# A chain of attention and two gated feed-forward layers: values stationary in attention's second product, and the first block's inputs cast straight from PSUM

## The chip, the core and the metric

The kernel runs on one core of one Trainium2 chip. The metric is the device time of one execution in microseconds (us), taken as the median of several runs. A core has five engines that run side by side and wait for each other by semaphores: TensorE (PE, matrix products; its weight loads are listed as PEld), VectorE (DVE), ScalarE (ACT), GpSimd (POOL) and SyncE (SP, which issues most transfers). TensorE reads the fast memory SBUF and writes to PSUM, eight banks of accumulators. A matmul has a stationary operand, which is loaded into the array first, and a moving one, whose columns stream through; the stationary operand's columns become the partitions of the result.

## What is computed

Local attention on 4 x 8 heads of 768 positions and 64 features, then two gated layers on the 3072 x 512 result. Cut to what matters:

```python
for c in range(nc):                       # 24 chunks of 32 queries
    k_full = concat([mem_k, k[l_start:r_end]])     # 8 + 16 + 32 + 8 = 64 keys
    v_full = concat([mem_v, v[l_start:r_end]])
    scores = scale * q_c @ k_full.T
    a = softmax(scores)
    out[c] = a @ v_full                   # the "second product": 32 queries x 64 features
x = out.transpose(0, 2, 1, 3).reshape(3072, 512)
x = (sigmoid(x @ w_gate) * (x @ w_val)) @ w_out    # 512 -> 1536 -> 512
h = x @ w_in                                       # 512 -> 2048 -> 512
return (h * sigmoid(h)) @ w_out2
```

## The kernel before

The tokens are cut into 24 tiles of 128 (t = 0 to 23), four to a block of 512. The products of the layers take x with its features on partitions, so that the input of a block is four pieces (KT = 4) of 128 features x 512 tokens, each split into a high and a low part (`fp32r`); three products of the parts make one product of nearly float32.

Attention of one tile goes through these steps. `att_scores` (or `att_scores_paired` for tiles 1 to 3) forms the scores with 64x32 (or 128x64) stationary pieces of q; `att_soften` takes the maximum off and forms the exponential; `att_sum` and `att_norm` divide by the sum; `att_turn` transposes the result on TensorE, so that keys lie on partitions, and ScalarE copies it to SBUF (`at`). `att_pv` is the second product: 4 chunks x 4 head groups x 2 halves make 32 float32 matmuls. Before, 32 queries of `at` are stationary and the 64 features of `vb` move, so that queries come out on partitions; `place` then transposes 32 x 32 blocks on VectorE into the block's `x32`, which has the features on partitions.

The order on each engine is written out by hand. Tiles 0 to 3 run in a prologue, whose order stands in the string `PROLOGUE` (`sc` scores, `max`, `sub`, `exp`, `sum`, `nm` normalise, `pt` turn, `px` second product, `tr` place; `idle` fills TensorE with matmuls that nobody reads; `rebias`, `join`, `high`, `rest` prepare the first weight units from a 64-bit format). Its `px` tiles share two PSUM buffers (`psp`) with the scores. After it `x_high` casts the four pieces of `x32` on ScalarE and `x_low` forms their low parts on VectorE; then the first projection (`proj_both`, tiles `pg` and `pv`) starts.

The other 20 tiles run beside the first layer. At fixed steps `run_events` issues a "meet" for tile t: the second product of tile t-1, directly behind it the scores of tile t, and then on VectorE the placing of t-1 and the softening of t. The second product and the scores lie in one PSUM tile `sx` of two banks. A last meet (t = 24) has only the second product. Everything TensorE does stands in one queue, so a meet stands between two projections (L360) or behind the output product (L104 to L108).

Of the kernel before, what the change touches and what calls it, by code (L numbers as in the profile page):

```python
# [15 lines left out]
P = 128  # L16
# [23 lines left out]
pt.0 sub.2 exp.2 sum.1 sc.3 nm.1 max.3 px.0 idle.1 sum.2 sub.3 exp.3 load.4 qk.4 nm.2 sum.3  # L40
pt.1 tr.0 rebias.0 pt.2 nm.3 px.1 tr.1 v.4 pt.3 join.0 rebias.1 px.2 px.3 idle.1
high.0 tr.2 tr.3 rest.0 join.1
# [15 lines left out]
def moe_kernel(ctx: ExitStack, tc: tile.TileContext, qh, kh, vh, wg, wv, wo, w2i, w2o, out):  # L58
# [237 lines left out]
    def att_pv(t, px, xt, off):  # L296

        at, vb = at_t.pop(t), v_t.pop(t)
        for c in range(4):
            for j in range(4):  # L300
                for a2 in range(2):
                    r = slice(a2 * 64, a2 * 64 + 64)
                    if t in PAIRED:
                        g = (2 * (c // 2) + j % 2) * P + (c % 2) * 2 * CH + (j // 2) * CH
                    else:
                        g = j * P + c * CH
                    o = px[j * CH : j * CH + CH, a2].rearrange("p (h x) -> p h x", h=2)
                    nc.tensor.matmul(  # L308
                        o[:, :, c * CH : c * CH + CH],
                        at[r, g : g + CH],  # L310
                        vb[r, (4 * c + j) * D : (4 * c + j + 1) * D],
# [4 lines left out]
        def place():  # L316
            nc.vector.transpose(
                out=xt[:, :, off : off + P].rearrange("p (u h) x -> p u h x", u=2),
                in_=px.rearrange("p u (h x) -> p u h x", h=2),
            )  # L320
# [5 lines left out]
    def x32_tile(name):  # L326
        return hold[0].tile([P, KT, 512], F32, tag="x32", name=name, bufs=2)
# [60 lines left out]
    with tc.manual_schedule():  # L388
# [115 lines left out]
        x32[0] = x32_tile("x32_0")  # L504
        steps, pts, last_exp = {}, {}, []
# [5 lines left out]
        def pro(what, i):  # L511
# [24 lines left out]
            elif what == "px":  # L536
                px = ps_p(f"px{i}")[:, :, :256]
                (steps["tr", i],) = att_pv(i, px, x32[0], i * P)
# [16 lines left out]
        psp_cm.__exit__(None, None, None)  # L555
        psy_cm = tc.tile_pool(name="psy", bufs=1, space=PSUM)
        psy.append(psy_cm.__enter__())
        src = x32.pop(0)
        x = [p1.tile([P, 2, 512], F32R, tag="x", name=f"x0_{kt}", bufs=5) for kt in range(KT)]

        def x_high(kt):
            nc.scalar.copy(x[kt][:, 0], src[:, kt])
# [17 lines left out]
        x_low(3)  # L580
        units[2].join()
# [17 lines left out]
        def run_events(i):  # L599
            for what, t in events.get(i, []):  # L600
                if what == "meet":
                    sx = ps_att(f"sx{t}")
                    steps = []
                    if t > n0:
# [3 lines left out]
                        steps += list(att_pv(t - 1, sx[:, :, 256:], x32[bn], jj * P))  # L608
# [657 lines left out]
        for bi, n in enumerate(BLOCKS1[:NB1]):  # L1266
# [3 lines left out]
            for f in range(NF1):  # L1270
# [21 lines left out]
                psg = (ps_y if first else ps_m)(f"pg{bi}_{f}")  # L1292
                if first:
                    psv = ps_y(f"pv{bi}_{f}")
# [81 lines left out]
def _layout(q, k, v, mem_k, mem_v, moe_w_gate, moe_w_val, moe_w_out, moe2_w_in, moe2_w_out):  # L1376
# [27 lines left out]
    def gv(w):  # L1404
        w = w.reshape(2, 2, 2, 2, 32, NF1, P)
        return w.transpose(5, 2, 0, 4, 1, 3, 6).reshape(NF1, P, KT * P)
# [39 lines left out]
```

## Time and profile before

| | |
|---|---|
| median of 3 runs | 1099.98 us (1099.97 to 1100.66) |
| the profiled execution | 1100.55 us |
| its span, first to last instruction | 1098.8 us |
| TensorE busy | 1085.0 us (99%) |
| VectorE busy | 758.0 us (69%) |
| ScalarE busy | 534.1 us (49%) |
| GpSimd busy | 95.0 us (9%) |

A profile is one execution. Shares of busy time are means over stages with different limits; the busy time of matmuls is modelled, so gaps are better read from start times. In the rows below a line such as L308 is line 308 of the kernel before, `out<-in` names the tiles with buffer numbers left out, and x64 is the number of instructions in a group. A float32 matmul is run as two passes, each with its own weight load.

### The profile page before, as it was taken

Reading aid. Unit: us, or ns where it says so; the run is one execution under the profiler, and the core shown is the slowest. Engines: PE = TensorE matmul, PEld = TensorE weight load, DVE = VectorE, ACT = ScalarE, POOL = GpSimd, SP = SyncE. Lnnn points to the kernel's source line nnn. Section 1 sums busy time; section 2 is a strip of 40 time slices with the busy share of each in tenths; the row PEclk is TensorE's granted clock in tenths of the full one; section 3 lists DMA queues with packets and bytes.
Section 4 is the critical chain, followed back from the end, with each engine's and each line's share of the span. In section 5 each row is a group of like instructions: output and inputs, shape, how many; then the busy total and the mean of one; then the engine's idle time right before and its main releaser. Section 6 shows DMA issues by size and latency. Waiting matters only on the chain.

```text
span 1098.8 us, 18989 instructions
## 1 busy us (share of the span) xinstructions
PE 1085.0 (99%) x7580; PEld 888.0 (81%) x7580; DVE 758.0 (69%) x1134; ACT 534.1 (49%) x791; POOL 95.0 (9%) x72
## 2 busy tenths in 40 slices
PE   7999999999999999999999999999999999999998
PEld 4888887888887788888778887888888888888887
DVE  7988877677666666667779967478734489443665
ACT  6767545455545453343445545455344445344542
POOL 0000001001000101011111001110011010011000
PEclk9999999999999999999999999999999999999999
DMA  8888788879788787689999599775665756655651
GB/s 313 272 290 303 265 299 263 289 278 331 291 276 302 257 286 275 231 288 353 339 330 363 182 300 315 265 288 207 233 201 201 274 191 227 210 191 209 218 213 68
DMA packets 106248, 288.03 MB, mean 262 GB/s; under 512 B 8624, under 2 KB 39344, under 8 KB 95408
## 3 DMA queue, kind: packets, MB, share of 16 engines
q1 hardware_dynamic: 105872, 286.43, 74.6%
q8 instruction: 60, 0.98, 0.4%
q10 hardware_dynamic: 288, 0.39, 0.1%
q14 instruction: 28, 0.23, 0.1%
HBM read 210.24 MB, written 76.55 MB: 261 GB/s over the span
## 4 chain that ended last, share of the span: by engine, by line
PE 94%; DVE 3%; ACT 1%; DMA 1%; issue 1%; DVEq 0%; ACTq 0%
PE o L1230 21%; PE c L1066 21%; PE pg L360 11%; PE pv L360 11%; PE y L104 4%; PE y L106 4%; PE y L108 4%; PE sx L308 1%; PE sx L220 1%; PE o_-1_1_6485 L1230 1%; PE o_-1_0_6484 L1230 1%; PE pt L292 1%; PE c_-1_5v L1066 1%; PE c_-1_4g L1066 1%; PE c_-1_3v L1066 1%; PE c_-1_2g L1066 1%
## 5 line engine op out<-in xcount | busy, mean ns | idle before, releaser
L1066 PE MATMUL c<-xp,wr 128*128 128x512 f32 x1008 | 229.6, 389 | 0.4 <-ACT s L1101 0.4
L1230 PE MATMUL o<-gf,wr 128*128 128x512 f32 x1008 | 229.0, 389 | 0.0
L1066 PEld LDWEIGHTS c<-xp,wr 128*128 128x128 f32 x1008 | 189.0, 188 | 40.4 <-ACT s L1101 1.2
L1230 PEld LDWEIGHTS o<-gf,wr 128*128 128x128 f32 x1008 | 189.2, 188 | 39.3
L360 PE MATMUL pv<-x,w 128*128 128x512 f32 x564 | 138.6, 394 | 0.0
L360 PE MATMUL pg<-x,w 128*128 128x512 f32 x564 | 136.4, 391 | 0.4 <-ACT x L96 0.4
L1173 DVE TENSOR_TENSOR gf<-g,gf 128x1024 fp32r<-128x1024 f32 x84 | 103.9, 1240 | 46.3 <-ACT gf L1169 45.9
L1169 ACT CAST gf<-g 128x1024 fp32r<-128x1024 f32 x84 | 88.1, 1053 | 86.8 <-PE o L1230 71.4
L360 PEld LDWEIGHTS pg<-x,w 128*128 128x128 f32 x564 | 105.2, 188 | 23.4 <-ACT x L96 1.5
L360 PEld LDWEIGHTS pv<-x,w 128*128 128x128 f32 x564 | 104.1, 188 | 23.2 <-DVE sg L375 0.5
L1031 DVE TENSOR_TENSOR s<-c,s 128x512 f32<-128x512 f32 x48 | 33.2, 691 | 56.7 <-PE c L1066 52.6
L1106 POOL TENSOR_TENSOR s<-s,s 128x512 f32<-128x512 f32 x24 | 34.3, 1431 | 321.7 <-ACT s L1105 321.7
L1034 DVE TENSOR_TENSOR g<-g,g 128x1024 f32<-128x1024 f32 x48 | 60.4, 1258 | 0.0
L370 ACT ACTIVATE sg<-pg 128x512 f32<-128x512 f32 x48 | 28.6, 596 | 60.1 <-PE pg L360 51.8
L380 DVE TENSOR_TENSOR g<-sg,g 128x512 fp32r<-128x512 f32 x48 | 33.2, 692 | 31.8 <-ACT g L377 31.8
L1037 ACT ACTIVATE g<-s 128x512 f32<-128x512 f32 x48 | 30.4, 632 | 50.9 <-DVE s L1031 50.9
L377 ACT CAST g<-sg 128x512 fp32r<-128x512 f32 x48 | 29.8, 620 | 49.3 <-DVE sg L375 49.3
L1031 DVE TENSOR_TENSOR u<-c,s 128x512 f32<-128x512 f32 x24 | 16.6, 690 | 51.8 <-PE c L1066 44.7
L269 ACT ACT_TABLE_LOAD x21 | 26.9, 1283 | 31.5 <-DVE e L261 29.7
L671 POOL TENSOR_TENSOR tcv<-w 128x512 f32<-128x512 f32 x12 | 16.7, 1415 | 284.2 <-DVE fcg L634 284.2
L104 PE MATMUL y<-g,wor 128*128 128x512 f32 x144 | 40.0, 400 | 0.0
L375 DVE TENSOR_TENSOR sg<-pv,sg 128x512 f32<-128x512 f32 x48 | 32.9, 685 | 8.5 <-PE pv L360 6.4
(603 smaller groups left out, 1600.8 us busy)
## 6 DMA issues: line engine op xcount, KB each, us to landing
wr<-w2o_d SPq DMA_DIRECT2D x42, 1024.0 KB, 4.9
wr<-w2i_d SPq DMA_DIRECT2D x24, 1024.0 KB, 5.5
wor<-wo_d SPq DMA_DIRECT2D x36, 512.0 KB, 6.6
wr<-w2i_d SPq DMA_DIRECT2D x24, 768.0 KB, 4.5
w2o_d<-coo SPq DMA_DIRECT2D x56, 256.0 KB, 6.9
w2i_d<-coi SPq DMA_DIRECT2D x24, 512.0 KB, 6.7
wr<-wc_d SPq DMA_DIRECT2D x12, 1024.0 KB, 6.5
v<-in_vh_dram SPq DMA_DIRECT2D x21, 512.0 KB, 5.4
```

The source lines that it names most:

```text
L104: nc.tensor.matmul(o, w_hi, x_hi, start=first, stop=False)
L106: nc.tensor.matmul(o, w_hi, x_lo, start=False, stop=False)
L108: nc.tensor.matmul(o, w_lo, x_hi, start=False, stop=last)
L360: nc.tensor.matmul(o[:, :n], w[:, pw, kt * P : (kt + 1) * P], x[kt][:, px, :n], start=i == 0, stop=i == len(steps) - 1,)
L380: nc.vector.tensor_tensor(out=g[:, 1, :n], in0=sg[:, :n], in1=g[:, 0, :n].bitcast(F32), op=ALU.subtract)
L1031: nc.vector.tensor_tensor(out=o, in0=a, in1=b_, op=ALU.add)
L1034: nc.vector.tensor_tensor(out=o, in0=a, in1=b_, op=ALU.subtract)
L1066: nc.tensor.matmul(o, w[:, pw, m, kt * P : (kt + 1) * P], X[i][:, px, kt], start=first and j == 0, stop=j == 5, skip_group_check=not first,)
L1106: nc.gpsimd.tensor_tensor(out=s5, in0=s5, in1=s1, op=ALU.add)
L1169: nc.scalar.copy(f[:, 0], src)
L1173: nc.vector.tensor_tensor(out=f[:, 1], in0=src, in1=f[:, 0].bitcast(F32), op=ALU.subtract)
L1230: nc.tensor.matmul(c[at[i], dp], w[:, pw, pl, dp * P : (dp + 1) * P], f[:, px, pl], start=i in (A11, S1, S2) and pp == 0 and j == 0, stop= ...
```

## The change

In `att_pv` the operands change places: the 64 features of `vb` are stationary (64 x 64), 32 queries of `at` move, and the features come out on partitions. The order of the matmuls goes round the four quarters of the array. `place` is now a copy. In the prologue `tr` and its transposes are gone; at `swap` the two score buffers are given up, and one PSUM tile of four banks takes the second products of all four tiles. The casts `x_high` and `x_low` read that tile; the first halves (256 tokens) of pieces 0 and 1 are cast on VectorE (`xa`). The order of the string changes accordingly: tile 0's product comes behind tile 1's turn, two fills stand where one stood, and the last fill goes. The pool of the output accumulators opens later, so the first two projections take other banks. The rows of the gate and value weights are laid out in another order on the host, to fit the new order of features.

```diff
@@ PROLOGUE
-pt.0 sub.2 exp.2 sum.1 sc.3 nm.1 max.3 px.0 idle.1 sum.2 sub.3 exp.3 load.4 qk.4 nm.2 sum.3
-pt.1 tr.0 rebias.0 pt.2 nm.3 px.1 tr.1 v.4 pt.3 join.0 rebias.1 px.2 px.3 idle.1
-high.0 tr.2 tr.3 rest.0 join.1
+pt.0 sub.2 exp.2 sum.1 sc.3 nm.1 max.3 idle.2 sum.2 sub.3 exp.3 load.4 qk.4 nm.2 sum.3
+pt.1 swap.0 px.0 rebias.0 pt.2 nm.3 px.1 v.4 pt.3 join.0 xa.0 xa.1 high.0 rebias.1 px.2 px.3
+rest.0 join.1
@@ att_pv
-            for j in range(4):
-                for a2 in range(2):
-                    r = slice(a2 * 64, a2 * 64 + 64)
+            for jj in range(2):
+                for ju, a2 in ((0, 0), (1, 1), (1, 0), (0, 1)):
+                    j, r = 2 * jj + ju, slice(a2 * 64, a2 * 64 + 64)
...
-                    o = px[j * CH : j * CH + CH, a2].rearrange("p (h x) -> p h x", h=2)
                     nc.tensor.matmul(
-                        o[:, :, c * CH : c * CH + CH],
+                        px[ju * D : ju * D + D, a2, jj, c * CH : c * CH + CH],
+                        vb[r, (4 * c + j) * D : (4 * c + j + 1) * D],
                         at[r, g : g + CH],
-                        vb[r, (4 * c + j) * D : (4 * c + j + 1) * D],
...
         def place():
-            nc.vector.transpose(
-                out=xt[:, :, off : off + P].rearrange("p (u h) x -> p u h x", u=2),
-                in_=px.rearrange("p u (h x) -> p u h x", h=2),
+            nc.vector.tensor_copy(
+                xt[:, :, off : off + P].rearrange("p (u h) x -> p u h x", u=2), px
             )
@@ the prologue's steps
-                px = ps_p(f"px{i}")[:, :, :256]
-                (steps["tr", i],) = att_pv(i, px, x32[0], i * P)
+                px = pxs[0][:, :, i * P : (i + 1) * P]
+                att_pv(i, px.rearrange("p (u h) x -> p u h x", u=2))
+            elif what == "swap":
+                psp_cm.__exit__(None, None, None)
+                psx_cm.append(tc.tile_pool(name="psx", bufs=1, space=PSUM))
+                psx = psx_cm[0].__enter__()
+                pxs.append(psx.tile([P, KT, 512], F32, tag="px", name="px"))
+            elif what == "xa":
+                nc.vector.tensor_copy(x[i][:, 0, : 2 * P], pxs[0][:, i, : 2 * P])
...
         def x_high(kt):
-            nc.scalar.copy(x[kt][:, 0], src[:, kt])
+            h = slice(2 * P if kt < 2 else 0, 4 * P)
+            nc.scalar.copy(x[kt][:, 0, h], src[:, kt, h])
@@ the first layer
-                psg = (ps_y if first else ps_m)(f"pg{bi}_{f}")
+                psg = (ps_y if (bi, f) == (0, 1) else ps_m)(f"pg{bi}_{f}")
...
-                    psv = ps_y(f"pv{bi}_{f}")
+                    psv = ps_m(f"pv{bi}_{f}")
```

On TensorE, in the prologue, from tile 3's scores to tile 1's second product: `pt` is a turn, `px` a second product, `warm` a fill; the shape is that of the result. Before:

```order
L240 MATMUL sc_249<-kv_96,qz_97 64x64 x15
L308 MATMUL px_276<-v_89,at_237 32x2x32 [waits DMAHW2_49,DVE_49,Activation_49]
L308 MATMUL px_276<-v_89,at_237 32x2x32 x31
L491 MATMUL warm<-ident 128x512
L292 MATMUL pt_236<-ident,e_w 128x128 [waits Activation_49] x4
L292 MATMUL pt_337<-ident,e_w 128x128 [waits DVE_49,Activation_49]
L292 MATMUL pt_337<-ident,e_w 128x128 x3
L308 MATMUL px_345<-kv_93,at_329 32x2x32 [waits DMAHW3_49]
L308 MATMUL px_345<-kv_93,at_329 32x2x32 x31
```

The same place after:

```order
L240 MATMUL sc_252<-kv_96,qz_97 64x64 x15
L489 MATMUL warm<-ident 128x512 x2
L292 MATMUL pt_239<-ident,e_w 128x128 [waits Activation_49] x4
L307 MATMUL px<-at_240,v_89 64x32 [waits DMAHW2_49,DVE_49,PE_49]
L307 MATMUL px<-at_240,v_89 64x32 x31
L292 MATMUL pt_344<-ident,e_w 128x128 [waits DVE_49,Activation_49]
L292 MATMUL pt_344<-ident,e_w 128x128 x3
L307 MATMUL px<-at_300,kv_93 64x32 [waits DMAHW3_49]
L307 MATMUL px<-at_300,kv_93 64x32 x31
```

Tile 0's second product has moved behind tile 1's turn, and two fills stand where it and one fill stood.

On VectorE, in the prologue, from tile 3's sum to the first weight unit's low part (`t_wg`, `w`), before:

```order
L278 RECIPROCAL r_325<-r_325 128x8 [waits DVE_49]
L317 STREAM_TRANSPOSE x_0_132<-px_276 128x4x128 [waits PE_49]
L287 TENSOR_TENSOR e_w<-e_w,r_325 128x512 [waits DVE_49]
L317 STREAM_TRANSPOSE x_0_132<-px_345 128x4x128 [waits PE_49]
L134 TENSOR_SCALAR stg_wg_126<-stg_wg_126 128x512 [waits DMAHW5_49]
L137 SCALAR_TENSOR_TENSOR t_wg_387<-stg_wg_126 128x512 [waits DVE_49,Activation_49]
L317 STREAM_TRANSPOSE x_0_132<-px_391 128x4x128 [waits PE_49]
L317 STREAM_TRANSPOSE x_0_132<-px_424 128x4x128 [waits PE_49]
L147 TENSOR_TENSOR w_458<-t_wg_387,w_458 128x512 [waits Activation_49]
```

and after:

```order
L278 RECIPROCAL r_296<-r_296 128x8 [waits DVE_49]
L287 TENSOR_TENSOR e_w<-e_w,r_296 128x512 [waits DVE_49]
L134 TENSOR_SCALAR stg_wg_126<-stg_wg_126 128x512 [waits DMAHW5_49]
L137 SCALAR_TENSOR_TENSOR t_wg_392<-stg_wg_126 128x512 [waits DVE_49,Activation_49]
L543 CAST x_0_132<-px 128x256 [waits PE_49]
L543 CAST x_1_133<-px 128x256
L147 TENSOR_TENSOR w_397<-t_wg_392,w_397 128x512 [waits Activation_49]
```

The four transposes are gone, and two half casts stand ahead of the weight unit's low part.

On TensorE, one meet in the main stretch, between the output product (`y`) and a gate projection (`pg`), before:

```order
L108 MATMUL y_3_649<-g_2_724,wo_738 128x512
L308 MATMUL sx_816<-v_379,at_765 32x2x32 [waits DMAHW4_49,Activation_49]
L308 MATMUL sx_816<-v_379,at_765 32x2x32 x31
L220 MATMUL sx_816<-k_606,q_605 32x64 [waits DMAHW5_49,DMAHW4_49]
L220 MATMUL sx_816<-k_606,q_605 32x64 x31
L360 MATMUL pg_4_906<-x_0_470,w_771 128x512 [waits Activation_49]
```

and after:

```order
L108 MATMUL y_3_647<-g_2_722,wo_736 128x512
L307 MATMUL sx_814<-at_763,v_384 64x32 [waits DMAHW4_49,Activation_49]
L307 MATMUL sx_814<-at_763,v_384 64x32 x31
L220 MATMUL sx_814<-k_604,q_603 32x64 [waits DMAHW5_49,DMAHW4_49]
L220 MATMUL sx_814<-k_604,q_603 32x64 x31
L358 MATMUL pg_4_904<-x_0_132,w_769 128x512 [waits Activation_49]
```

Nothing has moved there and no wait is new; the second product's results are 64 x 32 instead of 32 x 64.

## Rows read from the trace of the kernel before

**Rows 1.** The page: busy time by engine, and the chain that ended last.

```profile
PE 1085.0 (99%) x7580; PEld 888.0 (81%) x7580; DVE 758.0 (69%) x1134; ACT 534.1 (49%) x791; POOL 95.0 (9%) x72
...
PE 94%; DVE 3%; ACT 1%; DMA 1%; issue 1%; DVEq 0%; ACTq 0%
```

**Rows 2.** Windows: stretch, its length, busy us of each engine, clock, DMA.

```profile
24.00:34.00 10.00, 9.60 (x97) 6.87 (x99) 9.65 (x18) 8.26 (x15) 0.00 (x0) 1.00 0.76 247
34.00:130.00 96.00, 96.00 (x941) 78.94 (x926) 83.84 (x151) 65.53 (x106) 0.00 (x0) 1.00 0.81 280
...
240.00:440.00 200.00, 199.33 (x2040) 162.30 (x2039) 139.46 (x265) 96.87 (x149) 19.76 (x14) 1.00 0.83 292
```

**Rows 3.** TensorE's waits from 30 to 430: total us, times, longest.

```profile
PE pt L292 <- DVE e L287: 0.5, 2, 0.3
PE pg L360 <- ACT x L96: 0.4, 1, 0.4
```

**Rows 4.** Groups from 30 to 430: busy us, mean ns, idle before.

```profile
L308 PE MATMUL sx<-v,at 64*32 64x64 f32 x1280 | 17.2, 224 | 0.0
L317 DVE STREAM_TRANSPOSE x<-sx 128x512 f32<-128x512 f32 x20 | 14.3, 716 | 35.3 <-PE sx L220 32.1 <-PE sx L308 3.2
```

**Rows 5.** Timeline of TensorE, one meet: start, us, what.

```profile
56.73 0.86 PE L308 MATMUL sx<-v,at 64*32 64x64 f32 x64
57.39 0.85 PE L220 MATMUL sx<-k,q 64*32 64x64 f32 x64
58.17 0.50 PE L360 MATMUL pg<-x,w 128*128 128x512 f32 x1
```

**Rows 6.** Timeline of TensorE, 13.75 to 15.00: paired scores, first second product.

```profile
13.79 1.15 PE L240 MATMUL sc<-kv,qz 128*64 128x64 f32 x32 [0.96 <-ACT qz L207]
14.87 0.34 PE L308 MATMUL px<-v,at 64*32 64x64 f32 x15
```

**Rows 7.** Durations by line: ns min/median/max, starts, shape; loads and passes.

```profile
L308 PEld LDWEIGHTS sx<-v,at x1280: 102/106/108, 56.7 to 421.7; 64*32 64x32 f32 x183
...
L240 PEld LDWEIGHTS sc<-kv,qz x32: 133/138/138, 13.8 to 14.7; 128*64 128x64 f32 x32
L240 PE MATMUL sc<-kv,qz x32: 222/222/270, 13.8 to 14.7; 128*64 128x64 f32 x32
...
L360 PEld LDWEIGHTS pv<-x,w x11: 187/188/188, 300.0 to 302.3; 128*128 128x128 f32 x11
```

**Rows 8.** Groups by line and shape, as in rows 4: copies and half-width work.

```profile
L916 DVE COPY y<-y 128x512 f32<-128x512 f32 x8 | 5.1, 683 | 2.2 <-PE y L108 2.2
...
L261 DVE TENSOR_TENSOR e<-sc,m 128x256 f32<-128x256 f32 x2 | 0.8, 424 | 0.1
...
L269 ACT ACTIVATE e<-e 128x256 f32<-128x256 f32 x2 | 0.8, 416 | 3.3 <-DVE e L261 3.3
```

**Rows 9.** Timeline of the prologue: start, us, what, idle before.

```profile
18.47 0.66 PE L292 MATMUL pt<-ident,e_w 128*128 128x128 f32 x4 [1.17 <-ACT at L293]
...
19.05 0.86 PE L308 MATMUL px<-kv,at 64*32 64x64 f32 x64
...
19.61 0.65 DVE L287 TENSOR_TENSOR e_w<-e_w,r 128x512 f32<-128x512 f32 x1
...
20.40 0.63 PE L292 MATMUL pt<-ident,e_w 128*128 128x128 f32 x4 [0.49 <-DVE e_w L287]
...
22.09 1.13 PE L308 MATMUL px<-kv,at 64*32 64x64 f32 x92 [0.51 <-issue]
...
22.63 1.34 DVE L317 STREAM_TRANSPOSE x<-px 128x512 f32<-128x512 f32 x2 [0.63 <-PE px L308]
...
24.00 2.19 ACT L562 CAST x<-x 128x512 fp32r<-128x512 f32 x4 [1.28 <-DVE x L317]
...
24.67 2.30 PE L347 MATMUL pg<-x,w 128*128 128x512 f32 x8 [0.40 <-ACT x L562]
...
30.48 2.59 PEld L360 LDWEIGHTS pg<-x,w 128*128 128x128 f32 x12 [0.24 <-ACT w L144]
```

More of the change, by code (lines that the diff above doesn't have):

```diff
@@ L294, in att_turn, with att_pv @@
         at_t[t] = at
-    def att_pv(t, px, xt, off):
+    def att_pv(t, px, xt=None, off=0):
         at, vb = at_t.pop(t), v_t.pop(t)
         for c in range(4):
-            for j in range(4):
-                for a2 in range(2):
-                    r = slice(a2 * 64, a2 * 64 + 64)
+            for jj in range(2):
+                for ju, a2 in ((0, 0), (1, 1), (1, 0), (0, 1)):
+                    j, r = 2 * jj + ju, slice(a2 * 64, a2 * 64 + 64)
                     if t in PAIRED:
@@ L502, in ps_p @@
             return psp.tile([P, 2, 512], F32, tag="pp", name=name, bufs=2)
-        x32[0] = x32_tile("x32_0")
-        steps, pts, last_exp = {}, {}, []
+        steps, pts, last_exp, psx_cm, pxs = {}, {}, [], [], []
+        x = [p1.tile([P, 2, 512], F32R, tag="x", name=f"x0_{kt}", bufs=5) for kt in range(KT)]
         def behind(dma, other):
@@ L554, in moe_kernel @@
             pro(what, int(i))
[L555 to L559, printed above, removed]
+        src = pxs[0]
         def x_high(kt):
-            nc.scalar.copy(x[kt][:, 0], src[:, kt])
+            h = slice(2 * P if kt < 2 else 0, 4 * P)
+            nc.scalar.copy(x[kt][:, 0, h], src[:, kt, h])
         def x_low(kt):
@@ L580, in moe_kernel @@
         x_low(3)
+        psx_cm[0].__exit__(None, None, None)
+        psy_cm = tc.tile_pool(name="psy", bufs=1, space=PSUM)
+        psy.append(psy_cm.__enter__())
         units[2].join()
@@ L607, in run_events @@
                             x32[bn] = x32_tile(f"x32_{bn}")
-                        steps += list(att_pv(t - 1, sx[:, :, 256:], x32[bn], jj * P))
+                        px = sx[:, :, 256:].rearrange("p u (h x) -> p u h x", h=2)
+                        steps += list(att_pv(t - 1, px, x32[bn], jj * P))
                         prefetch_v(t)
@@ L1405, in gv @@
         w = w.reshape(2, 2, 2, 2, 32, NF1, P)
-        return w.transpose(5, 2, 0, 4, 1, 3, 6).reshape(NF1, P, KT * P)
+        return w.transpose(5, 0, 3, 4, 1, 2, 6).reshape(NF1, P, KT * P)
     w2i = moe2_w_in.reshape(KT, P, NF2, P).transpose(2, 1, 0, 3)
```

## The prediction

> **What bounds the kernel now.** I read the page first, then the table of windows, then the groups by line, and last single stretches of the timeline. The page says TensorE: matmuls fill 99% of the span, and the chain that ended last is 94% TensorE [rows 1]. VectorE is busy 69%, ScalarE 49%. The windows show where attention lies: between 34 and 440 us, beside the first product, and there TensorE is busy in practically all of the time, at a clock granted in full [rows 2]. So whatever the edit does to VectorE in that stretch costs or gives nothing directly; whatever it does to TensorE's time counts in full. TensorE's own waits there come to 0.9 us [rows 3], which is all the slack that could swallow anything. Only the first 24 us are different: there the chain passes through several engines.
>
> **The second product in the main stretch.** Twenty tiles (t = 4 to 23) have their second product in the main stretch, at "meet". Before, each is 32 float32 matmuls that the hardware runs as 64 passes, with a 64x32 stationary and 64 streamed columns, on eight parts of the array side by side; 1280 passes in all [rows 4]. One meet in time order [rows 5]: the first pass at 56.73, the scores of the next tile at 57.39, the next projection at 58.17. So 64 passes take 0.66 us when work of the same shape follows.
>
> After, there are again 64 passes, but the stationary is 64x64 and 32 columns stream. Streaming halves, the weight load doubles, and there are four parts of the array instead of eight, so each part does 16 passes in a row where it did 8. What does a pass of such a part cost? The nearest row is the paired scores of the prologue [rows 6]: 16 matmuls with 64 stationary columns on two half arrays, so also 16 passes in a row on each, with 64 streamed columns. Their 32 passes take 1.15 us less the 0.22 us that one lasts [rows 7], 0.93 us from first to last start, 58 ns per pass. There load and stream are equally wide, so the row alone doesn't say which of them paces it. The weight loads say it: a load of 32 columns is recorded with 106 ns, of 64 columns with 138 ns, of 128 columns with 188 ns [rows 6, 7]. That is 0.85 to 1.0 ns per column, thus 55 to 64 ns for 64 columns: about the whole 58 ns. A load can run beside the stream of the pass before (in the paired scores load and stream together would be over 110 ns), but not beside another load of the same part. So I take 16 passes at the load's pace: 0.93 us, plus 0.01 us for two more parts. Against the 0.64 us from first to last start before (0.86 less the 0.22 of the last pass [rows 5]), that is +0.29 us a tile. The bounds: if loads cost nothing, the pace of the first starts before applies: that row was cut at 15.00 us, and its 15 passes start within 0.34 less 0.22 us, 0.12 us [rows 6]; 64 would need 0.51 us, so -0.13 us a tile; if load and stream add up (55 and 29 ns), 16 times 84 ns is 1.35 us, so +0.7 us. I take +0.29 because the paired scores are the only row with this load width and the same number of passes on a part. 20 x 0.29 = **+5.8 us**.
>
> What the trace shows here is 32 ns more for 32 more columns. The Trainium skill ("TensorE: Matmul & The Clock Gate", section "LDWEIGHTS (loading the stationary operand)") says that a load goes by the number of stationary columns and not by the rows, columns divided by 1.2 in ns; by it 64 columns would be 53 ns and the term about 0.9 us of load per tile. The trace agrees, and this rule speaks against the change: it makes the wide operand the one that is loaded.
>
> **A change of shape in mid-meet.** Before, second product and scores have one shape, and the scores start right behind. The scores' own 64 passes, though, take 0.78 us until a full-array matmul may start (57.39 to 58.17 [rows 5]). The same 64 passes followed by their own shape take 0.66. So a change of shape costs 0.12 us. After, 64x64 is followed by 64x32: one more change in each of 19 meets (the last, t = 24, has no scores behind it). The last pass streams only half, which gives back some 0.02 us: 0.10 us each. Bounds: nothing, if these two shapes don't count as different, and 0.12 us. I take 0.10, since every change in the trace costs about that: 19 x 0.10 = **+1.9 us**.
>
> **VectorE's transposes.** A transpose of 0.716 us becomes a copy [rows 4]; a copy of the same size from PSUM takes 0.683 us [rows 8]. That is 0.03 us x 20 on an engine with idle time, and nothing on the path: VectorE waits there for TensorE, 32 us in 16 waits [rows 4]. What is queued behind the copy on VectorE (maximum, subtraction of the next tile's scores) comes up to 0.4 us later, and TensorE reads its result only at the turn, four steps on. Price nothing; if that cover were gone, TensorE's 0.5 us of waiting at the turn [rows 3] would grow.
>
> **The prologue.** Here four things change. (a) Before, the last second product ends at 23.22, two transposes run to 23.97, the first cast to about 24.6, and the first projection starts at 24.67 [rows 9]. After, the casts read PSUM, so the two last transposes go, and the first cast covers 256 columns (a ScalarE pass of that width takes 0.42 us [rows 8]) instead of 512 (about 0.6): 1.45 us of TensorE's wait becomes 0.45. (b) The first two transposes also go from VectorE, so the normalisation that ran at 19.61 starts some 0.5 us sooner, and tile 3's turn (20.40) with it, unless the longer second product of tile 1 holds it: it starts at 19.05 [rows 9], and 19.05 + 0.93 + 0.12 is 20.10, so 0.3 us remain. (c) Four products are each 0.29 us longer. The first now waits for the score buffers (VectorE reads tile 3's scores last) and fits into the 1.17 us gap before 18.47 [rows 9] with 0.1 us to spare. The last two stand in a row: +0.58 us. (d) In between lies a stall of 0.51 us that the profile calls "issue" [rows 9], in the middle of tile 2's product. The instructions ahead of it are nearly the same number, so I leave it where it is; if it is bound to a point in time rather than to work done, it eats (b). So the last product ends between 22.8 and 23.6, the casts start 0.4 to 1.2 us earlier than at 24.00. Behind them stands VectorE's queue, which is full from 24 to 34 us (9.65 of 10 us [rows 2]): low parts, then the third weight unit, and the projection at 30.48 waits for that unit's cast [rows 9]. By VectorE's queue I get 29.4 to 30.0 for it. So the prologue gives 0.5 to 1.1 us; with the stall fixed in time I take **-0.6 us**, bounds -1.5 (also the stall gone) and +0.3 us (the first product overruns its gap).
>
> The two added half casts on VectorE (0.42 us each [rows 8]) stand where it waited 0.63 us for the third transpose, so they are inside this figure. The buffers of the first projections move to other banks, which nobody waits for until TensorE has passed three projections: nothing.
>
> **Sum.** +5.8 +1.9 -0.6, less 0.4 us that TensorE's waits of 0.9 us may swallow: **+6.7 us**. The profiled execution took 1100.55 us for a span of 1098.8; the median of the runs is 1099.98. Added to the median: **1106.7 us**.
>
> **The rivals.**
> - *Loads paced, no price for the change of shape* (the two 64-row shapes pass for one): +5.8 -0.6 -0.4, 1104.8 us. For it: both leave the row split alone. Against it: every change of shape in the trace costs 0.12 us.
> - *Passes limited by how fast instructions come*. The 64 passes before start in 0.64 us though eight parts at 58 ns each would need 0.47. If that supply limits the new form too, the second product stays at 0.64 us and only the change of shape remains: +1.9 -0.6 -0.4, 1100.9 us. Against it: 0.93 us of loads on each part.
> - *The other side: faster.* Loads of different parts and of one part overlap fully, so 64 passes need 0.51 us; 20 x -0.13 = -2.6, no price for the shape, prologue -1.2: 1096.2 us. It decides as soon as a pass of one part costs below some 32 ns. Against it the load's 138 ns against 106.
> - *Load and stream add up.* If two quarters that share rows can't load while one of them streams, a pass costs 84 ns: 20 x 0.7 + 1.9 - 0.6, 1115 us. Against it the paired scores, where both halves share all rows and still keep 58 ns a pass. The Trainium skill (same page, section "Part 3: Packing small matmuls", what overlaps) says that loads run beside matmuls in flight only in another row group, which would be this case. The trace differs, so it gets little.
>
> **How the numbers follow.** Forecast 0.58, no price for the shape 0.14, supply 0.14, faster 0.08, load plus stream 0.06. The forecast's own range is 1105.0 to 1108.5: 0.25 to 0.31 us a tile, 0.05 to 0.12 for the shape, prologue -1.5 to +0.3. To hold 8 in 10 it takes in the first rival and the upper half of the second: 1101.0 to 1108.5. 0.2% is 2.2 us, about what a measurement of this kernel can tell from no change; by it forecast, first and last rival are slower (0.78), supply is the same (0.14), and the remaining rival is faster (0.08).
>
> **What would show it.** In the profile after, a meet's second product should show 64 passes with loads near 138 ns, from first to next line about 1.05 us instead of 0.66, and the scores' 0.78 us unchanged. If the loads are at 106 ns or the stretch stays at 0.66 us, my main term is wrong. TensorE's busy time between 34 and 440 us should stay whole, and the same lines stand later by 0.4 us more with each meet; if later lines catch up, there was slack that I didn't see. The first projection should start 0.5 to 1.4 us before 24.67, and the one at 30.48 by 0.5 to 1.1 us sooner. VectorE's copy should be near 0.68 us.

## The result and the profile after

The changed kernel takes 1109.28 us (median of 6 runs, 1109.01 to 1109.47), the kernel before beside it 1100.32 us (6 runs, 1099.85 to 1100.76). The ratio is 1.0081, 95% interval 1.0068 to 1.0094: slower by 9.0 us. The forecast was 1106.7 with a range to 1108.5; the time lies 0.8 us above the range. Of the 2.6 us to the forecast, 0.3 are the kernel before, which took 1100.32 us beside this one and 1099.98 in the runs that the forecast was added to. The profiled execution took 1109.47 us for a span of 1107.7, so 8.9 us of span are to be found.

The page of the changed kernel gives the busy time of each engine; below it are two rows of its table of windows (stretch, length, busy us, clock), for the stretch with attention, and TensorE's waits from 30 to 440:

```profile
PE 1094.1 (99%) x7580; PEld 896.2 (81%) x7580; DVE 757.5 (68%) x1132; ACT 533.3 (48%) x791; POOL 94.3 (9%) x72
```

```profile
34.00:130.00 96.00, 96.00 (x955) 79.02 (x935) 82.03 (x149) 64.14 (x104) 0.00 (x0) 1.00 0.79 275
240.00:440.00 200.00, 199.35 (x2081) 162.56 (x2079) 135.80 (x258) 95.22 (x145) 21.64 (x16) 1.00 0.83 293
```

```profile
PE pt L292 <- DVE e L287: 0.5, 2, 0.3
PE pg L358 <- ACT x L96: 0.4, 1, 0.4
```

TensorE's busy time grows by 9.1 us [rows 1], it stands as full as before at the same clock [rows 2], and its two waits are what they were, to the tenth [rows 3]. So the added time is TensorE's own work, and no slack took any of it.

One meet in the timeline of TensorE (start, us, what), then the durations of the second product's loads and passes (ns min/median/max), then VectorE's copy:

```profile
56.95 1.14 PE L307 MATMUL sx<-at,v 64*64 64x32 f32 x64
58.01 0.86 PE L220 MATMUL sx<-k,q 64*32 64x64 f32 x64
58.80 3.04 PE L358 MATMUL pg<-x,w 128*128 128x512 f32 x12
```

```profile
L307 PEld LDWEIGHTS sx<-at,v x1280: 129/135/135, 56.9 to 430.5; 64*64 64x64 f32 x183
L307 PE MATMUL sx<-at,v x1280: 219/219/241, 56.9 to 430.6; 64*64 64x32 f32 x183
```

```profile
L316 DVE COPY x<-sx x20: 692/693/693, 58.9 to 430.8; 128x512 f32<-128x512 f32 x20
```

From the second product's first line to the scores it is 1.06 us now and was 0.66 [rows 5]; the scores take 0.79 us, where they took 0.78. A load takes 135 ns in place of 106 [rows 7]. Taken from the single starts in the trace, the 64 passes start within 0.916 us (before 0.642), and from the last of them to the first of the scores it is 0.149 us (before 0.017). The first meet starts 0.215 us later than before, the last one 8.50 us later, so 19 meets added 0.436 us each. The span comes together like this:

| piece | forecast | measured |
|---|---|---|
| second product, 20 meets | +5.8 | 20 x 0.274 = +5.5 |
| change of shape, 19 meets | +1.9 | 19 x 0.132 = +2.5 |
| the rest of a meet | 0 | 19 x 0.03 = +0.6 |
| prologue | -0.6 | +0.2 |
| swallowed by TensorE's waits | -0.4 | 0 |
| sum | +6.7 | +8.8 |

The pieces of a meet are medians of the single starts. Of the 0.03 us, 0.01 is in the scores (0.632 to 0.642 us). The other 0.02 lies between the meets: from the first projection behind a meet to the next meet it is 17.02 to 17.04 us before and 17.07 after in most meets of equal length. Why those projections take longer, no run tells.

The timeline of the prologue after, over all engines, with the idle time before a row and what ended it in brackets:

```profile
20.30 0.69 DVE L137 SCALAR_TENSOR_TENSOR t_wg<-stg_wg 128x512 int32<-128x512 int32 x1
...
20.91 0.75 DVE L543 CAST x<-px 128x256 fp32r<-128x256 f32 x2
...
21.71 2.07 PE L307 MATMUL px<-at,kv 64*64 64x32 f32 x128 [0.92 <-DVE x L543]
...
23.85 0.65 ACT L564 CAST x<-px 128x256 fp32r<-128x256 f32 x2 [1.32 <-PE px L307]
...
24.27 1.20 PE L345 MATMUL pg<-x,w 128*128 128x512 f32 x4 [0.49 <-ACT x L564]
24.53 0.69 DVE L567 TENSOR_TENSOR x<-px,x 128x512 fp32r<-128x512 f32 x1 [0.73 <-ACT x L564]
25.25 1.07 ACT L564 CAST x<-px 128x512 fp32r<-128x512 f32 x2 [0.76 <-DVE x L567]
25.89 1.23 PE L345 MATMUL pg<-x,w 128*128 128x512 f32 x4 [0.42 <-ACT x L564]
...
26.36 0.69 DVE L567 TENSOR_TENSOR x<-px,x 128x512 fp32r<-128x512 f32 x1 [1.14 <-ACT x L564]
...
30.69 0.30 PEld L358 LDWEIGHTS pg<-x,w 128*128 128x128 f32 x2 [0.27 <-ACT w L144]
```

Two waits are new. The products of tiles 2 and 3 stand ready and wait 0.92 us for VectorE's half casts of tiles 0 and 1 (L543), which read the PSUM tile that these products write, and which stand in VectorE's queue behind a weight step (L137). And in what follows, ScalarE's casts (L564) and VectorE's low parts (L567) take turns. A low part needs the cast of its own piece, but the first one waits 0.73 us, until the second cast is done too; the third cast needs no low part and waits 0.76 us for one, and the second low part, whose cast is done, waits 1.14 us for the third and fourth cast. In the trace these are waits for semaphores: the third cast carries one for VectorE's, which the first low part raises. What casts and low parts share is that both read that one PSUM tile. The wait for an instruction of 0.51 us in the middle of tile 2's product [rows 9] is gone. The first projection starts at 24.27 in place of 24.67, but the one whose loads began at 30.48, called the second projection below, now starts at 30.69.

### The profile page after: what moved, and what is told of

Its sections match the earlier page's. It is cut to its first block, busy times and chain, and to the rows that moved or that the text cites. A ratio compares the mean times of both kernels' runs of the same rounds, so it can differ in the third digit from the quotient of the medians.

```text
span 1107.7 us, 18991 instructions
## 1 busy us (share of the span) xinstructions
PE 1094.1 (99%) x7580; PEld 896.2 (81%) x7580; DVE 757.5 (68%) x1132; ACT 533.3 (48%) x791; POOL 94.3 (9%) x72
## 4 chain that ended last, share of the span: by engine, by line
PE 94%; DVE 3%; ACT 1%; DMA 1%; issue 1%; SPq 0%; DVEq 0%; ACTq 0%
PE o L1236 21%; PE c L1072 20%; PE pg L358 11%; PE pv L358 11%; PE y L104 4%; PE y L106 4%; PE y L108 4%; PE sx L307 2%; PE sx L220 1%; PE o_-1_1_6483 L1236 1%; PE o_-1_0_6482 L1236 1%; PE c_-1_2g L1072 1%; PE c_-1_5v L1072 1%; PE c_-1_4g L1072 1%; PE c_-1_3v L1072 1%; PE c_-1_1v L1072 1%
## 5 line engine op out<-in xcount | busy, mean ns | idle before, releaser
L316 DVE COPY x<-sx 128x512 f32<-128x512 f32 x20 | 13.9, 693 | 44.0 <-PE sx L220 40.4
```

## The experiments

In the following, "second product" is the time from the first to the last start of a meet's passes, "gap" that from its last start to the first of the scores, both from the single starts.

### Which half costs what

`main_only` takes the prologue and the weights' order of the kernel before and the new second product from tile 4 on; `prologue_only` takes the other halves. In each, the rows of the weights fit the features' order of the first block alone.

```diff
     def att_pv(t, px, xt, off):
         at, vb = at_t.pop(t), v_t.pop(t)
+        if t >= 4:
+            px4 = px.rearrange("p u (h x) -> p u h x", h=2)
...
+                            px4[ju * D : ju * D + D, a2, jj, c * CH : c * CH + CH],
+                            vb[r, (4 * c + j) * D : (4 * c + j + 1) * D],
+                            at[r, g : g + CH],
```

> The prologue of the kernel before (old form and transposes for tiles 0 to 3), the new form and the copy only in the 20 meets of the main stretch; the blocks of this kernel disagree on the order of features, so it shows time alone. Theory A (the meets cost the time: 0.92 us of second product instead of 0.64, and 0.13 us for the change of shape, 20 and 19 times): the second product starts 0.28 us later relative to its end, a meet grows by 0.42 us, in sum +8.2 to +8.6 us, 1108.5 to 1109.0. Theory B (part of the loss comes from the prologue's later start, which shifts loads against the first layer): below 1107.

> The new prologue (tiles 0 to 3 in the new form, casts from PSUM), the old form and the transposes in the 20 meets; here too the blocks disagree on the order of features, so it shows time alone. Theory A: the new prologue gains nothing, because tile 2's second product waits for VectorE's half casts and the casts wait for the low parts: the second projection starts at 30.7 as in the changed kernel (30.48 before), the time is 1100.3 to 1100.7. Theory B (the prologue gains its 0.6 us and the meets cost 9.5 us): 1099.7, the second projection at 29.9.

`main_only`: 1108.95 us (1108.12 to 1109.57), ratio 1.0077 (1.0064 to 1.0089), second product 0.916, gap 0.149 us. `prologue_only`: 1100.92 us (11 runs, 1100.66 to 1101.68), ratio 1.0006 (0.9997 to 1.0015), second product and gap as before; the second projection starts 16.88 us after tile 3's scores, as in the changed kernel, where it was 16.71 before. So the first expectations come true, the time of `prologue_only` 0.2 us above its range. The meets cost 8.6 us by themselves, and the new prologue brings nothing. In the time, its loss is within the interval; in the traces it is plain: all seven kernels with this prologue start the second projection 16.87 to 16.88 us after tile 3's scores, the two with the old one (`before`, `main_only`) 16.7.

### What paces the second product

Four kernels change the width of one operand. `wide_stream` streams 64 columns in place of 32 (the second half falls on a neighbour's place). `half_load` and `half_rows` load 32 of the 64 features; they differ in how the rows are placed. `split_load` makes two matmuls of each, with 32 features.

```diff
@@ wide_stream
+                    w = CH if t < 4 else 2 * CH
+                    g, o = min(g, 512 - w), min(c * CH, P - w)
...
-                        px[ju * D : ju * D + D, a2, jj, c * CH : c * CH + CH],
+                        px[ju * D : ju * D + D, a2, jj, o : o + w],
...
-                        at[r, g : g + CH],
+                        at[r, g : g + w],
@@ half_rows
+                    w, o = (D, ju * D) if t < 4 else (D // 2, ju * D // 2)
...
-                        px[ju * D : ju * D + D, a2, jj, c * CH : c * CH + CH],
-                        vb[r, (4 * c + j) * D : (4 * c + j + 1) * D],
+                        px[o : o + w, a2, jj, c * CH : c * CH + CH],
+                        vb[r, (4 * c + j) * D : (4 * c + j) * D + w],
@@ half_load, place
+            for lo in (0, D):
+                nc.vector.tensor_copy(xv[lo : lo + 32], px[lo : lo + 32])
+                nc.scalar.copy(xv[lo + 32 : lo + D], px[lo : lo + 32])
@@ split_load
+                    for d in (0, 32) if t >= 4 else (0,):
+                        w = D if t < 4 else 32
...
+                            px[ju * D + d : ju * D + d + w, a2, jj, c * CH : c * CH + CH],
+                            vb[r, (4 * c + j) * D + d : (4 * c + j) * D + d + w],
```

> The changed kernel, but in the 20 meets each second product streams 64 columns instead of 32 (neighbouring columns are computed twice; the result is not used for more than its time). Loads stay 64 wide. Theory A (the load of the next weights paces a pass, the stream runs beside it): the 64 passes stay at 0.92 to 0.94 us from first to last start; the time within 0.6 us of the changed kernel, 1109.0 to 1109.9. Theory S (load and stream add up on a part, or the stream paces): 0.92 us grows by 0.2 to 0.5 us, 1113 to 1119.

> The changed kernel, but in the 20 meets only 32 of the 64 feature columns are stationary (the other half of the features is left out; VectorE and ScalarE copy the computed half twice). Still four parts, 16 passes each, 32 streamed columns. Theory A (loads pace): the loads show 103 to 107 ns, the 64 passes need 0.5 us, or 0.64 if instructions limit them as before the change; the shape is now that of the scores, so they follow after 0.02 us; the time falls by 7 to 10 us to 1099 to 1102. Theory P (four parts instead of eight are the cause, whatever is loaded): 0.92 us stays, only the 2.5 us of the shape go, 1106.5.

> The changed kernel, but from tile 4 on only 32 of the 64 features are loaded per pass, into contiguous rows 0 to 63; one VectorE copy of 64 partitions places them, GpSimd fills the other rows with zeros once per block (half of attention's features are left out). Same passes, same four parts, no added work on VectorE or ScalarE. Theory A (the load's columns pace the second product, the change of shape costs 0.13 us): second product 0.50 to 0.60 us from first to last start, gap to the scores under 0.05 us, so 20 x 0.35 + 19 x 0.10 = 9 us less than the changed kernel: 1100.2 us (1099.5 to 1101). Theory B (the added time is not the loads', but four parts in place of eight or the order of the passes): second product stays at 0.9 us, time stays above 1107 us.

> The changed kernel, but from tile 4 on each matmul is split into two with 32 features each: 128 passes on eight parts with a narrow load. If a part's loads set the pace (16 narrow loads on each of eight parts), 0.53 to 0.60 us from first to last start and about 1102 us. If the old form's 64 passes in 0.64 us are the pace at which passes are supplied, 10 ns each, 128 need 1.28 us: 20 x 0.36 more than the changed kernel, less 19 x 0.13 for the shape that no longer changes, about 1114 us.

The measured second products, with the scores of a further kernel (`wide_scores`, below) as a last row; ns a pass is the time divided by the passes less one:

| kernel | loaded columns | streamed | parts | passes | us | ns a pass | gap |
|---|---|---|---|---|---|---|---|
| before | 32 | 64 | 8 | 64 | 0.642 | 10.2 | 0.017 |
| half_rows | 32 | 32 | 4 | 64 | 0.563 | 8.9 | 0.045 |
| split_load | 32 | 32 | 8 | 128 | 1.097 | 8.6 | 0.045 |
| after | 64 | 32 | 4 | 64 | 0.916 | 14.5 | 0.149 |
| wide_stream | 64 | 64 | 4 | 64 | 0.943 | 15.0 | 0.148 |
| wide_scores, scores | 64 | 64 | 4 | 64 | 0.984 | 15.6 | |

Times: `wide_stream` 1109.98 us (1109.61 to 1110.27), ratio 1.0087 (1.0072 to 1.0102); `half_rows` 1099.78 us (11 runs, 1099.56 to 1100.33), ratio 0.9997 (0.9989 to 1.0006); `half_load` 1119.56 us (1119.02 to 1120.07), ratio 1.0174 (1.0159 to 1.0189); `split_load` 1150.12 us (1147.98 to 1151.17), ratio 1.0452 (1.0437 to 1.0466).

Twice as many streamed columns add 0.027 us to a meet, all of it between the fourth and the fifth pass (in the time 0.7 us, 0.1 above the first expectation, with intervals of the ratio that overlap); half as many loaded columns take 0.353 us away, and with them the whole loss: `half_rows` is at the time of the kernel before. A meet of `half_rows`, and its loads, in the trace:

```profile
56.75 0.76 PE L308 MATMUL sx<-at,v 64*32 64x32 f32 x64
57.36 0.85 PE L220 MATMUL sx<-k,q 64*32 64x64 f32 x64
...
```

```profile
L308 PEld LDWEIGHTS sx<-at,v x1280: 102/106/110, 56.7 to 420.9; 64*32 64x32 f32 x183
L308 PE MATMUL sx<-at,v x1280: 192/193/213, 56.7 to 420.9; 64*32 64x32 f32 x183
```

The loads are back at 106 ns, and from line to line it is 0.61 us. That the four parts stayed and the time went shows that it isn't the number of parts by itself.

`half_load` has the same second product (0.564) and gap (0.045), but I expected 1099 to 1102 us and it took 1119.56. Its TensorE waits from 30 to 440 show where (total us, times, longest):

```profile
PE pv L360 <- DVE sg L375: 4.4, 4, 1.6
PE pg L360 <- ACT x L96: 3.6, 3, 2.4
PE pt L292 <- DVE e L287: 2.7, 9, 0.7
PE sx L308 <- ACT at L293: 0.9, 2, 0.4
```

Its placing makes four copies of 0.6 to 0.7 us on two engines out of one, and TensorE then waits 11.6 us for VectorE and ScalarE in place of 0.9. That is 10.7 of the 19.2 us by which its span is longer than that of `half_rows`; the rest stands in no listed wait. The time of this run says nothing of the loads; it is why `half_rows` was made, whose placing is one copy.

`split_load` refutes both of its expectations: 128 passes start within 1.097 us, so 10 ns a pass is no floor, and its eight parts don't reach the pace of four (16 passes on a part take 0.56 us with four parts, 1.1 us with eight).

The single starts tell two limits apart. With 64 loaded columns on four parts, four passes, one to each part, start 6 to 7 ns apart, and the next comes 38 ns later: a round every 58 ns, in `after` and `wide_stream` alike. The paired scores [rows 6], with 64 columns on two halves, have the same round, 58 to 59 ns for two passes, and the turns (L292), with 128 columns on the whole array, start 109 ns apart. So there a part goes at a pace of its own, by its loaded columns. With 32 loaded columns the passes settle, on four parts and on eight, to two in every 16 to 17 ns: a pace that all of them share.

The time of `split_load` is far above 1114 us for another reason. The second meet in TensorE's timeline, then all its waits from 50 to 440 that are called "issue":

```profile
78.43 1.29 PE L309 MATMUL sx<-at,v 64*32 64x32 f32 x128
79.57 0.80 PE L220 MATMUL sx<-k,q 64*32 64x64 f32 x59
82.27 0.31 PE L220 MATMUL sx<-k,q 64*32 64x64 f32 x5 [1.90 <-issue]
```

```profile
PE sx L220 <- issue: 18.5, 7, 4.5
PE pv L360 <- issue: 6.3, 2, 4.8
```

After 187 recorded short passes in a row TensorE stands still for 1.90 us and waits for no semaphore that the profile shows ("issue"); nine such halts make 24.8 us, and a tenth of 1.97 us follows at 449.8.

The trace's DMA records tell more. Queue q8, which the page lists as "instruction", moves one packet of 16 KB at a time. It has 60 of them in the kernel before, which has 15160 recorded passes and loads of TensorE, and 70 in `split_load`, which has 17720: 253 for each packet in both. And all fifteen halts of over 0.4 us that the profile calls "issue", here, in the prologue of the kernel before and of `main_only`, and in a kernel below (`old_main_split_first`), end 1.2 to 1.6 us after such a packet has landed. So TensorE most likely stood waiting for its own instructions; no run changes their transfer alone, so this is read from the times and not shown by an experiment.

Around the ends of the six longest halts the granted clock falls too; one window of that stretch (columns as above; the clock is the third number from the end, 0.97 as a mean of the levels of 2.4 and 1.2 GHz):

```profile
200.00:300.00 100.00, 89.39 (x1247) 72.48 (x1245) 60.91 (x117) 43.23 (x66) 7.56 (x6) 0.97 0.74 251
```

### The change of shape

`wide_scores` gives the scores 64 loaded columns too, so that the shape no longer changes within a meet (64 queries are loaded where 32 belong).

```diff
-                    g = (4 * a + c) * CH
+                    g, w, o = (4 * a + c) * CH, CH, c * CH
+                    if t >= 4:
+                        g, w, o = (4 * a + c // 2 * 2) * CH, 2 * CH, c // 2 * 2 * CH
...
-                        sc[c * CH : c * CH + CH, u, a],
-                        qb[r, g : g + CH],
+                        sc[o : o + w, u, a],
+                        qb[r, g : g + w],
```

> The changed kernel, but the scores of the 20 tiles in the main stretch also have 64 stationary columns (two chunks' queries at once against one chunk's keys; the scores are wrong in half of the rows, the time is what counts). Then second product and scores have one shape. Theory A (the gap of 0.149 us between them is the change of shape): it falls to about 0.02 us, while the scores' passes grow from 0.64 to 0.92 us: 20 x 0.28 less 19 x 0.13, +3.0 us, 1112.3. Theory D (the gap is the drain of the wide loads, whatever follows): 0.149 us stays, 1114.8.

It took 1114.26 us (1113.96 to 1114.5), ratio 1.0125 (1.0108 to 1.0142). The time lies nearer to the second expectation, but the gap decides: it falls from 0.149 to 0.038 us, so the change of shape is what costs most of it. The scores, with 64 columns to load, grow from 0.642 to 0.984 us, which is 0.06 more than I expected; 20 x 0.34 less 19 x 0.11 is 4.7 us, and the time rose by 5.0. That the scores grew more than I expected is most of why the time passed the first expectation. In its timeline:

```profile
57.27 1.14 PE L309 MATMUL sx<-at,v 64*64 64x32 f32 x64
58.22 1.20 PE L222 MATMUL sx<-k,q 64*64 64x64 f32 x64
59.35 2.81 PE L360 MATMUL pg<-x,w 128*128 128x512 f32 x11
```

### The prologue

`no_half_casts` leaves VectorE's half casts away, so that ScalarE casts the whole pieces. `four_tiles` gives each piece a PSUM tile of its own in place of one tile for all. `four_tiles_no_half` does both.

```diff
@@ no_half_casts
-pt.1 swap.0 px.0 rebias.0 pt.2 nm.3 px.1 v.4 pt.3 join.0 xa.0 xa.1 high.0 rebias.1 px.2 px.3
+pt.1 swap.0 px.0 rebias.0 pt.2 nm.3 px.1 v.4 pt.3 join.0 high.0 rebias.1 px.2 px.3
...
-            h = slice(2 * P if kt < 2 else 0, 4 * P)
+            h = slice(0, 4 * P)
@@ four_tiles
-                pxs.append(psx.tile([P, KT, 512], F32, tag="px", name="px"))
+                for k in range(KT):
+                    pxs.append(psx.tile([P, 512], F32, tag=f"px{k}", name=f"px{k}"))
```

> The changed kernel without the two half casts on VectorE; ScalarE casts all four pieces whole. Theory A (tile 2's second product waited for these casts because they read the same PSUM tile): it starts near 20.7 instead of 21.71, a stall called issue may come back and take up to 0.5 us of that; the last second product ends 0.5 to 1.0 us sooner, but each of the first two casts is 0.2 us longer and casts still take turns with low parts: the second projection at 30.1 to 30.5 instead of 30.69, the time 1108.7 to 1109.1. Rival (the wait is for the instructions or for tile 2's weights of the turn): tile 2's second product stays at 21.7.

> The changed kernel with four PSUM tiles for the first block instead of one, and the half casts on VectorE kept. Theory A: tile 2's second product still waits for the half casts (start near 21.7), since they read two of the tiles that it writes, but casts and low parts no longer take turns: the second projection at 29.8 to 30.3, the time 1108.5 to 1109.0.

> As no_half_casts, and the four banks of the first block's results are four PSUM tiles instead of one. Theory A (casts and low parts take turns because they read one PSUM tile): the four casts run back to back, about 2.4 us in a row, the low parts beside them; the second projection at 29.4 to 30.0, the time 1108.0 to 1108.6. Rival (the turns come from VectorE's queue, not from the shared tile): casts and low parts as in no_half_casts, the same time.

From the start of tile 3's scores to the first and second projection (first matmul of each), and the times:

| kernel | first | second | us | ratio |
|---|---|---|---|---|
| before [rows 6, 9] | 10.88 | 16.71 | 1100.3 | |
| after | 10.46 | 16.88 | 1109.28 | 1.0081 |
| no_half_casts | 9.69 | 16.32 | 1109.11 (1108.53 to 1109.27) | 1.0078 (1.0065 to 1.0092) |
| four_tiles | 10.20 | 15.80 | 1108.50 (1108.14 to 1108.56) | 1.0073 (1.0058 to 1.0088) |
| four_tiles_no_half | 9.55 | 15.31 | 1108.25 (1107.27 to 1108.36) | 1.0069 (1.0056 to 1.0081) |

TensorE's timeline of `no_half_casts`, and ScalarE's casts:

```profile
20.25 2.07 PE L307 MATMUL px<-at,kv 64*64 64x32 f32 x128
23.02 1.21 PE L345 MATMUL pg<-x,w 128*128 128x512 f32 x4 [0.70 <-ACT x L564]
24.85 1.22 PE L345 MATMUL pg<-x,w 128*128 128x512 f32 x4 [0.62 <-ACT x L564]
```

```profile
24.21 1.07 ACT L564 CAST x<-px 128x512 fp32r<-128x512 f32 x2 [0.76 <-DVE x L567]
```

and of `four_tiles_no_half`:

```profile
20.10 2.07 PE L311 MATMUL px<-at,kv 64*64 64x32 f32 x128
22.74 2.19 PE L349 MATMUL pg<-x,w 128*128 128x512 f32 x8 [0.57 <-ACT x L568]
```

```profile
22.10 2.06 ACT L568 CAST x<-px 128x512 fp32r<-128x512 f32 x4 [0.21 <-PE px L311]
```

Without the half casts the product of tile 2 no longer waits; with four tiles and the half casts it still waits 0.58 us for them, as expected. Without the shared tile the four casts run in a row, wait for TensorE alone and overlap with the low parts, and the first projection isn't cut in two. So both first theories hold, and the rivals fall; in the two kernels with four tiles the second projection came a little earlier still than I expected. Both together put the second projection 1.57 us earlier than in the changed kernel and 1.40 earlier than before. The two causes are shown by these starts. In the time it is 1.0 us of 1109.28, with intervals that overlap.

### Is there a version that beats both?

`old_main_four_tiles` joins the second product of before, from tile 4 on, to the prologue of `four_tiles_no_half`. `old_main_split_first` also splits the prologue's products into 32 features, so that their order fits the old weights.

```diff
@@ old_main_split_first, prologue
+                    for h in range(2):
+                        nc.tensor.matmul(
+                            px[2 * a2 + h][j * CH : j * CH + CH, c * CH : c * CH + CH],
+                            vb[r, (4 * c + j) * D + h * CH : (4 * c + j) * D + h * CH + CH],
+                            at[r, g : g + CH],
```

> The kernel before in the main stretch (second product and transposes as before), the changed prologue with four PSUM tiles and without the half casts. Time only: the first token block's features stand in the new order and the others' in the old one, while the weights fit only the first. If the prologue's gain of 1.4 us at the second projection goes through to the end, 1098.9 us (1098.5 to 1099.4). If a later wait swallows it, 1100.0 to 1100.5 us.

> As old_main_four_tiles, but the prologue's products are split into 32 features each (128 passes), so that the features come out in the old order and the weights stay as before: a whole kernel. If a split product takes 1.28 us and not 0.92, the two that stand in a row at the end are 0.7 us later, so half of the gain remains: 1099.6 us (1099.0 to 1100.4). If narrow loads make it 0.6 us, it gains 2 us: 1098.3 us.

`old_main_four_tiles` took 1099.35 us (11 runs, 1098.79 to 1099.78) beside 1099.98, ratio 0.9993 (0.9984 to 1.0002). In its trace the second projection is 1.2 us earlier than before (15.49 us after tile 3's scores), and the last meet still is (419.96 in place of 421.14); the span is 0.9 us shorter. The time lies at the upper end of the first expectation's range, and the interval of the ratio holds no gain as well as the whole one. `old_main_split_first` took 1111.36 us (1110.39 to 1112.41), ratio 1.0099 (1.0083 to 1.0114), far from what I expected. TensorE's timeline:

```profile
19.48 0.62 PE L328 MATMUL px<-at,kv 64*32 64x32 f32 x39
21.84 1.43 PE L328 MATMUL px<-at,kv 64*32 64x32 f32 x89 [1.74 <-issue]
...
27.59 1.88 PE L328 MATMUL px<-at,kv 64*32 64x32 f32 x128 [2.80 <-issue]
32.53 1.47 PE L328 MATMUL px<-at,kv 64*32 64x32 f32 x94 [3.06 <-issue]
```

The same halts as in `split_load`: 7.6 us in three. In this stretch, up to 34 us, the granted clock is 0.82, where it was full before. So none of the kernels here that compute the whole beats the one before.

## Why the prediction came out as it did

**What bounds the kernel, and the sign: right.** `main_only` alone gives 8.6 of the 9.0 us, and TensorE stays as full as before.

**The second product, +0.29 us a tile: right, in size and in its account.** Measured 0.274, by loads of 135 ns where I read 138 from the paired scores. That the load and not the stream sets the pace is shown by `wide_stream` and `half_rows`, which also refute the rival in which load and stream add up (a pass on a part would have grown by 29 ns with the doubled stream; it grew by 1.7 on average). "16 passes in a row on each part" at 58 ns each is what the single starts show, a round of four passes every 58 ns, and the paired scores were the right row: the same 58 ns on two halves. The account ends where loads are narrow. There a pace that all passes share sets in, some 8.3 ns a pass, on four parts and on eight. The rival that was to be faster falls with the measured +0.274.

**The rival of supply: refuted, and half true.** In short runs 128 passes come at 8.6 ns each, faster than the 10.2 ns that I took for a possible limit. But in long runs of short passes the supply does stop, for microseconds. The 0.51 us in the profile before [rows 9] looks like such a halt: it ends 1.4 us after a packet of q8 has landed. I left it where it was without an account.

**The change of shape, +0.10 us: mis-sized.** The gap grew by 0.132 us and the scores by 0.01. The 0.02 us that I took off because the last pass streams only half isn't there: `wide_stream`, which streams all 64, has the same gap. `wide_scores` (64 columns, then 64: 0.038) and `half_rows` (32, then 32: 0.045) show that the gap goes with the change in the loaded columns, so the rival without a price for it falls as well. Of the terms with bounds this is the only one that left them: they ended at 0.12, the gap grew by 0.132. With the 0.02 us a meet that lies between the meets it comes to 3.1 us instead of 1.9.

**The prologue, -0.6 us: the step that failed, and the largest miss.** It turned out +0.2. The forecast that the transposes go and the first projection starts earlier came true (0.4 us), but the sum counted the half casts as "inside this figure" because VectorE has the time. It is not VectorE's time that they cost: the products of tiles 2 and 3 write the tile that they read, so TensorE waits for them, 0.92 us, and what VectorE does first (a weight step) stands before that. The other unseen wait is the turn-taking of casts and low parts on one PSUM tile, 0.76 and 1.14 us in the rows above; before, the two engines read one SBUF tile, `x32`, and the four casts ran in a row [rows 9]. The halt of 0.51 us went, as in the lower bound of -1.5 us, and the two waits ate more than it gave. `no_half_casts` and `four_tiles_no_half` show it: without the two waits the second projection comes 1.4 us earlier than before. The upper bound, +0.3 us, held, but for the wrong cause (an overrun of tile 0's product).

**Swallowed slack, -0.4 us: wrong.** No row had given this term. The waits at the turn and at the projection are as long as before [rows 3]: what TensorE waits for there was itself released by TensorE's earlier work, so both moved along together. That reading is argued from the equal rows, not shown by a run of its own.

**VectorE, nothing: right.** The copy takes 0.693 us (I read 0.68), and nobody waits for it.

Had the prologue been put at +0.2 and the slack at nothing, the sum would have been +7.9, 1107.9 us, still inside the range. Of the 1.4 us from there to 1109.28, the change of shape with what lies between the meets makes 1.2 and the kernel before, at 1100.32 in place of 1099.98, 0.3; the second product, 5.5 for 5.8, takes 0.3 off, and 0.2 stay open. The lower end of the forecast's own range doesn't follow from its bounds: they add up to +4.0 us, 1104.0 and not 1105.0.

## What to carry to other kernels

When the operands of a small matmul change places, count the loaded columns before the streamed ones: here, on four parts, 32 more loaded columns cost 5.6 ns a pass and 32 more streamed ones 0.4, and neighbours in TensorE's queue with unlike loaded widths cost 0.11 to 0.13 us more at a seam than neighbours with like ones. When a step is changed to read an accumulator directly, list who writes that same tile next and who else reads it; one tile for everything turned a copy saved into two waits, and four tiles took them back. Work taken off an engine with idle time, as the transposes were here, brings nothing by itself; what counts is what the bounding engine does, and what it waits for.

## What the runs showed of the chip

Runs of short matmuls can outpace what feeds TensorE: after 187 passes at about 9 ns it stood still for 1.9 us, in other places for up to 4.8 us, and each of the fifteen halts ended 1.2 to 1.6 us after a 16 KB packet of the instruction queue had landed; kernels with 64 passes and 64 scores in a row showed no such halt in the meets. With 32 loaded columns the number of array parts in use (four or eight) made no difference to the pace of passes (8.9 and 8.6 ns). With 64 it did: a part took a pass every 58 ns, so two parts gave 29 ns a pass (the paired scores) and four 14.5; with 128 columns on the whole array it was 109 ns (the turns). And two engines that only read one PSUM tile were made to take turns, by waits for each other's semaphores; with a PSUM tile for each piece the four casts ran in a row, beside low parts that read other tiles. Whether the memory would need the turns on one tile, no run here tells.
